# A planned two-layer kernel on one core: a one-element copy on another engine, another table of step order, and two buffers handed out differently

## The chip, the cores and the metric

The kernel runs on one core of a Trainium2 chip, which has eight. The metric is the device time of one execution in microseconds, as a median over several runs. A core has five engines that run side by side and wait for one another by semaphores: TensorE (PE: matmuls; PEld: weight loads), VectorE (DVE), ScalarE (ACT), GpSimd (POOL) and SyncE (SP). The last three can also issue DMA transfers. Each engine does its instructions strictly in the order in which they were issued to it: an instruction that waits holds up all that are queued behind it.

## The reference

Two layers on x of 2048 rows by 512 columns in bf16, each with its layer norm and its residual. The first is attention with 32 heads of 16 columns, in which each row sees 8 rows: itself and those 2, 4, ... 14 rows before it. The second is a gated network of width 1376.

```python
def _A_ref(x, wqkv, wo):
    H = 32; Dh = D // H
    W, dil = 8, 2
    q, k, v = qkv[0], qkv[1], qkv[2]
    idx = pos[:, None] - (jnp.arange(W) * dil)[None, :]
    ...
    logits = jnp.where(mask, einsum("bhsd,bhswd->bhsw", q, kg) * Dh ** -0.5, -1e9)
    o = einsum("bhsw,bhswd->bhsd", softmax(logits), vg)
    return o @ wo

def _B_ref(x, W_gate, W_up, W_down):
    gate, up = x @ W_gate, x @ W_up
    return ((gate * (gate > 0)) * up) @ W_down

h = x + _A_ref(_layernorm(x), wqkv, wo)
h2 = h + _B_ref(_layernorm(h), W_gate, W_up, W_down)
```

## The kernel before

The 2048 rows are worked in four chunks of 512. For each chunk `tk` the kernel makes the same steps, and a planner (`Plan`) interleaves the steps of all four. A step is one call of `add`: an engine, an assumed duration, the steps it depends on, the buffers that it takes and uses, and a function that issues its instructions. A step is named here as in the code, with its chunk behind a point: `xst.1` is the step `xst` of chunk 1. Steps of the first chunk's first layer norm also carry their block of 128 rows: `xxn1.0`.

The steps of a chunk, in the order of the data:

- First layer norm: `xst`, `xag` (VectorE, L473 and L476: statistics of one block of 128 rows and their aggregate), `xrl`, `xre` (ScalarE, L486 and L490: 1/sqrt by a logarithm and an exponential), `xnb` (VectorE, L494), `xxn` (the normalized rows; VectorE L521 in chunk 0, ScalarE L518 in the others). The rows are then turned so that columns lie on partitions: in chunks 0, 1 and 2 by TensorE (`xtp`, L550) and a copy out of PSUM (`xte` on ScalarE, L566; `xtv1` on VectorE, L564), in chunk 3 by DMA transposes on SyncE (`xtd`, L539, tile `quad<-row`).
- Query, key and value: twelve products of four matmuls each on TensorE (`qkv0` to `qkv11`, L591) and as many copies out of PSUM on ScalarE (`qe0` to `qe11`, L599). In chunk 0 the first six are cut by rows and by halves of the weights into `qka`, `qkd`, `qkb`, `qkc`, `qke`, so that they can begin when only a part of the input is there; `qka` and `qkd` need the first two of the four parts of the query and key weights, which `setup` loads with the transfers of L325 and L340.
- Scores: the products of queries and shifted keys on VectorE (`pr0`, `pr1`, L642; in chunk 0 in halves, L657: eight of them), summed over a head's columns by matmuls (`sc0`, `sc1`, L648, or after an addition on VectorE, `pa`, L692), the exponential on ScalarE (`ex0`, `ex1`, L706), and in chunk 0 a mask on VectorE (`mk0`, `mk1`, L709). `es` (VectorE, L738) adds the two halves, `den` (TensorE, L723) sums them, `dl` and `dr` (ScalarE, L729 and L732) make the reciprocal, and `am0`, `am1` (VectorE, L750) multiply by it in chunks 1 to 3.
- The weights of the attention are spread over the heads' columns by DMA broadcasts on SyncE: `bd0S` and `bd1S`, four transfers each (L766, tile `big<-ex`).
- `mu0` to `mu3` (VectorE, L798; in halves in chunk 0, L813) multiply them with shifted values. The eight products are then added in three levels; the first is an accumulating DMA on GpSimd (`ta`, L841, tile `big<-big`) for all but one of the sixteen, the others are on VectorE (`tree`, L801 and L835). In chunk 0 `om` (L805) multiplies by the reciprocal.
- The output projection `wo0` to `wo3` (TensorE, L879), the residual `rs` (VectorE, L890), the second layer norm (`hnm` L456, `hsq` L462, `hxn` L516; transposes `htp` or `htd`; `hrl` and `hre` make the factor that the very last step multiplies by).
- The gated network: `mm` (TensorE, L952 and L919), the copies out of PSUM `ue` and `ge` (ScalarE, L956 and L959), their product `gu` (VectorE, L980 and L929; `gtd` turns the last 96 columns by DMA), the second product `dn` (TensorE, L1002), the result `o` (ScalarE L1008 in chunks 0 and 1, followed by an accumulating DMA `oa`, L1031; VectorE L1010 in chunks 2 and 3) and the output transfer `os`. In the last chunk the last block of 128 rows is done in three parts of 256, 128 and 128 columns.

What sets the order is the list `RANK` (L18): its n-th entry is the rank of the n-th step that was added. `Plan.order` sorts by it, so on every engine the steps go out by rising rank. The planner's clock, with its assumed durations and arrival times (`XT`, `WT`), then says which buffer of a ring a step gets, and in which order the steps of different engines are written into the program; no instruction carries a time.

Three places beside the order play a part:

- The up and down weights are loaded late (`LATE`), because their place in SBUF must not be written too early. A tiny step `lg` (L859) writes four elements into the place of the up weights once the attention output of chunk 0 is complete; the transfers `ldu` (SyncE, L315) wait for it.
- `hsq` squares the centred rows on ScalarE; only the sum (`accum_out`) is used, and the squares go to a tile `junk` (L295) that nobody reads.
- The results `o` of chunks 2 and 3 go through a ring of five row buffers (`o_s`, L285), shared with two other uses.

Of the kernel before, what the change touches and what calls it, by code (L numbers as in the profile page):

```python
# [8 lines left out]
P = 128  # L9
# [50 lines left out]
class Op:  # L60
# [4 lines left out]
    def __init__(self, eng, dur, fn, deps=(), prio=0.0, take=(), use=(), lat=0.0, dq=None):  # L65
        self.eng, self.dur, self.fn, self.lat, self.dq = eng, dur, fn, lat, dq
        self.deps = [d for d in deps if d is not None]
        self.prio, self.take, self.use = prio, list(take), list(use)
        self.start = self.done = None


class Slots:
# [130 lines left out]
def kernel(  # L203
# [11 lines left out]
    nc = tc.nc  # L215
# [868 lines left out]
```

## Time and profile before

| | us |
|---|---|
| median of 3 runs | 195.03 |
| lowest and highest run | 194.85, 195.93 |
| the profiled execution, its own time | 195.59 |
| its span, from the first to the last instruction | 193.6 |
| TensorE, VectorE, ScalarE, GpSimd busy | 185.8, 150.2, 115.8, 22.9 |

The mean granted TensorE clock was 0.997. The profile is read in these views, all of the one profiled execution:

- the page's busy table (engine, busy time, share of the span, number of instructions), and its table of groups: line, engine, operation, what is written and read, shape, count, then busy time, the mean length of one in ns, and idle time ahead of it;
- the waits: an engine with tile and line, what it waited for, then the total in us, the number of waits and the longest;
- the chain of work that ended last: start, length, and what the time went to;
- the timeline: start, length, engine and line, operation, shapes, count of merged instructions; in brackets the idle time of the engine ahead of it and what ended that. "SPq" is SyncE's queue while it issues transfers;
- stretches: for each the length, then for TensorE, weight loads, VectorE, ScalarE and GpSimd the busy time with the count of instructions, then the clock, the share of the DMA engines, and GB/s;
- the answer for one tile or line: count, shortest, median and longest duration in ns, first and last start in us; for transfers the time from issue to landing.

A matmul of 512 columns is shown longer than the distance to the next, since matmuls are pipelined.

### The profile page before, as it was taken

What the parts mean: (1) busy time and instruction counts of PE and PEld (TensorE: products, weight loads), DVE (VectorE), ACT (ScalarE), POOL (GpSimd) and SP (SyncE); (2) the same over time, 40 slices, a digit from 0 to 9 for tenths busy, and PEclk for the clock granted to TensorE, in tenths of its full rate; (3) what the DMA queues carried; (4) which work ended last, traced back from release to release, by engine and by line L of the source; (5) the groups of instructions that cost most, each with busy time, mean ns of one, the idle gap of its engine ahead of it and who ended that gap; (6) DMA issues with size and microseconds to landing.
All of it is one profiled execution on the core that took longest, in us unless ns stands there. A gap on an engine that the chain in (4) does not pass through costs nothing.

```text
span 193.6 us, 3051 instructions
## 1 busy us (share of the span) xinstructions
PE 185.8 (96%) x1120; PEld 95.9 (50%) x1120; DVE 150.2 (78%) x245; ACT 115.8 (60%) x236; POOL 22.9 (12%) x35
## 2 busy tenths in 40 slices
PE   7599999899999999999999999999999999999993
PEld 7487454465446444544444445444554444554542
DVE  6699979999999999999999987898575720224343
ACT  3579897985839397861183798034595613475800
POOL 3000000330530033000064000017000000000000
PEclk9999999999999999999999999999999999999998
DMA  5898166795048859985559944759911150113013
GB/s 195 272 375 317 36 157 117 148 199 112 3 125 259 224 141 192 179 252 112 108 95 196 219 91 96 174 105 188 198 31 27 22 140 0 39 45 108 0 60 106
DMA packets 26734, 26.44 MB, mean 137 GB/s; under 512 B 12544, under 2 KB 22624, under 8 KB 26720
## 3 DMA queue, kind: packets, MB, share of 16 engines
q1 hardware_dynamic: 23264, 16.39, 30.9%
q0 software_dynamic: 2736, 8.91, 24.8%
q10 hardware_dynamic: 720, 0.95, 1.4%
q8 instruction: 9, 0.15, 0.3%
q14 instruction: 5, 0.04, 0.1%
HBM read 8.42 MB, written 2.10 MB: 54 GB/s over the span
## 4 chain that ended last, share of the span: by engine, by line
PE 82%; DMA 7%; ACT 5%; issue 2%; DVE 1%; SPq 0%; DVEq 0%
PE bank L952 35%; PE bank L591 16%; PE bank L1002 15%; PE bank L879 7%; PE bank L648 3%; DMA x_sm<-in_A_x_dram 3%; DMA quad<-row 3%; PE bank L919 3%; PE bank L550 2%; ACT vT L599 1%; DMA out_dram<-row 1%; ACT junk L462 1%; ACT row L518 1%; DVE row L1010 1%; ACT gr L959 1%
## 5 line engine op out<-in xcount | busy, mean ns | idle before, releaser
L952 PE MATMUL bank<-quad,wgu_sb 128*128 128x512 bf16 x320 | 71.9, 379 | 0.0
L952 PEld LDWEIGHTS <-wgu_sb 128*128 128x128 bf16 x320 | 30.9, 98 | 37.0 <-issue 1.3
L1002 PE MATMUL bank<-wd_sb,gT 128*128 128x512 bf16 (+3 forms) x198 | 39.4, 356 | 0.0
L956 ACT CAST up_sb<-bank 128x512 bf16<-128x512 f32 x40 | 22.7, 592 | 20.9 <-PE bank L952 11.7
L591 PE MATMUL bank<-quad,wqk_sb 128*128 128x512 bf16 (+2 forms) x176 | 29.9, 321 | 0.9 <-DMA quad<-row 0.9
L959 ACT ACTIVATE gr<-bank 128x512 bf16<-128x512 f32 x40 | 23.2, 606 | 9.5 <-PE bank L952 5.9
L980 DVE TENSOR_TENSOR gT<-gr,up_sb 128x1024 bf16<-128x1024 bf16 x20 | 13.8, 689 | 19.3 <-ACT gr L959 17.1
L1002 PEld LDWEIGHTS <-gT 128*128 128x128 bf16 (+1 forms) x198 | 18.4, 98 | 20.1 <-issue 0.4
L642 DVE TENSOR_TENSOR big<-quad,kT 128x4096 bf16<-128x4096 bf16 x11 | 24.9, 2289 | 0.1
L798 DVE TENSOR_TENSOR big<-big,vT 128x4096 bf16<-128x4096 bf16 x10 | 22.5, 2289 | 0.5 <-DMA big<-ex 0.5
L591 PEld LDWEIGHTS <-wqk_sb 128*128 128x128 bf16 x176 | 17.0, 113 | 11.5 <-issue 1.2
L841 POOL DMA_DIRECT2D big<-big x13 | 12.5, 985 | 63.8 <-DVE nb L494 31.6
L591 PE MATMUL bank<-quad,wv_sb 128*128 128x512 bf16 x64 | 16.0, 380 | 0.0
L879 PE MATMUL bank<-wo_sb,quad 128*128 128x512 bf16 x64 | 15.3, 380 | 0.0
L1008 ACT ACTIVATE up_sb<-bank,iv 128x512 bf16<-128x512 f32 x8 | 5.1, 684 | 16.3 <-PE bank L1002 16.3
L801 DVE TENSOR_TENSOR big<-big 128x1024 bf16<-128x1024 bf16 (+2 forms) x19 | 12.1, 660 | 3.4 <-DMA big<-big 3.3
L890 DVE SCALAR_TENSOR_TENSOR x_sm<-x_sm,bank 128x512 bf16<-128x512 bf16 x16 | 10.7, 683 | 3.0 <-PE bank L879 3.0
L462 ACT ACTIVATE junk<-x_sm,mv 128x512 bf16<-128x512 bf16 x16 | 11.7, 731 | 1.5 <-DVE mv L456 1.5
L473 DVE BATCH_NORM_STATS2 st<-x_sm 128x6 f32<-128x512 bf16 x16 | 10.1, 682 | 2.0 <-DMA x_sm<-in_A_x_dram 2.0
L813 DVE TENSOR_TENSOR big<-big,vT 128x2048 bf16<-128x2048 bf16 x8 | 9.3, 1219 | 1.4 <-DMA big<-ex 1.4
L599 ACT CAST quad<-bank 128x512 bf16<-128x512 f32 x16 | 9.1, 590 | 2.1 <-PE bank L591 2.1
L518 ACT ACTIVATE row<-x_sm,nb,rs 128x512 bf16<-128x512 bf16 x12 | 9.8, 815 | 0.3 <-DVE nb L494 0.3
(80 smaller groups left out, 173.6 us busy)
## 6 DMA issues: line engine op xcount, KB each, us to landing
big<-big POOLq DMA_DIRECT2D x13, 512.0 KB, 5.9
big<-ex SPq DMA_DIRECT2D x32, 128.0 KB, 2.8
wgu_sb<-in_B_W_gate_dram SPq DMA_DIRECT2D x2, 688.0 KB, 9.9
wgu_sb<-in_B_W_up_dram SPq DMA_DIRECT2D x2, 688.0 KB, 4.7
wd_sb<-in_B_W_down_dram SPq DMA_DIRECT2D x2, 640.0 KB, 4.6
x_sm<-in_A_x_dram SPq DMA_DIRECT2D x2, 512.0 KB, 5.9
wqk_sb<-wqk_sb POOLq DMA_DIRECT2D x2, 512.0 KB, 6.6
x_sm<-up_sb POOLq DMA_DIRECT2D x4, 256.0 KB, 4.9
```

What stands on the lines that cost most here:

```text
L462: nc.scalar.activation(out=junk[:], in_=h.t[:] if h else x_sm[:, tk * BPC + j, :], func=ACT.Square, bias=mv.t[:, j, 0:1], scale=1.0, accum ...
L591: nc.tensor.matmul(mm.t[:, lo:hi], lhsT=wv_sb[:, dt, t:D:NT] if c == 2 else wqk_sb[:, dt, c * D + t:(c + 1) * D:NT], rhs=xnT.t[:, dt, lo:h ...
L642: V.tensor_tensor(out=pb.t[:].rearrange("p (t w) s -> p t w s", t=2), in0=q4, in1=k4, op=ALU.mult)
L798: V.tensor_tensor(out=mt.t[:], in0=ab.t[:], in1=v8, op=ALU.mult)
L801: V.tensor_tensor(out=mt.t[:, 0:n, :], in0=mt.t[:, 0:n, :], in1=mt.t[:, n:2 * n, :], op=ALU.add)
L841: nc.gpsimd.dma_start(mt.t[:, 0:4, :], mt.t[:, 4:8, :], accum_op=ALU.add)
L879: nc.tensor.matmul(od.t[:], lhsT=OT.t[:, t, j * P:(j + 1) * P], rhs=wo_sb[:, t, :], start=(t == 0), stop=(t == NT - 1 and tk not in RPE))
L952: nc.tensor.matmul(mm.t[:fs, lo:hi], lhsT=wgu_sb[:, dt, g, ft * P: ft * P + fs], rhs=hnT.t[:, dt, lo:hi], start=(dt == 0), stop=(dt == NT ...
L956: nc.scalar.copy(out=ub.t[:fs, i, :], in_=um.t[:fs, :])
L959: nc.scalar.activation(out=gr.t[:fs, i, :], in_=gm.t[:fs, :], func=ACT.Relu)
L980: V.tensor_tensor(out=gt.t[:fs, 0:n, :], in0=gr.t[:fs, 0:n, :], in1=ub.t[:fs, 0:n, :], op=ALU.mult)
L1002: nc.tensor.matmul(od.t[:, c0:c1], lhsT=gts[ft].t[:fs, ft % 2, j * P:(j + 1) * P], rhs=wd_sb[:fs, ft, c0:c1], start=(ft == 0), stop=(ft == ...
```

## The change

Four things in the program are different.

1. `lg`, the four-element copy that releases the transfer of the up weights, is on VectorE instead of GpSimd.
2. `RANK` is another list. Of each engine's queue some steps are where they were and most have moved; the first ones, and the places that matter later, are listed below.
3. `junk` has two halves, and `hsq` writes them in turn.
4. In chunks 2 and 3 a result takes a row buffer per block of 128 rows; so the three parts of the last block share one, where each had its own.

In the planner, `order` with a list takes one step at a time over all engines, where it took the lowest rank of each engine and among these the earliest by its clock. Its model knows two more waits, for the landing of the eighth transfer before (`hw`, `flight`) and between some key copies and score products (`near`), and has other arrival times in `XT` and `WT`. These bear on which buffer a step gets and on the order of writing, not on the instructions.

```diff
 RANK = [
     1, 2, 3, 4, 5, 6, 7, 8, 9, 10, 18, 11, 12, 13, 14, 15, 16, 17, 0, 19,
-    21, 23, 24, 27, 31, 34, 35, 20, 26, 28, 32, 37, 40, 44, 49, 22, 25, 30, 33, 39,
+    21, 24, 26, 29, 33, 37, 36, 20, 22, 25, 27, 31, 35, 40, 39, 23, 28, 30, 32, 44,
...
@@ def order
-        waiting = list(self.ops)
+        self.flight = [9.0, 9.4, 11.5, 12.9, 14.9, 16.2, 17.9, 19.6]
+        waiting = sorted(self.ops, key=lambda o: (o.prio, o.seq), reverse=True) if RANK else list(self.ops)
...
-            for op in ([q[-1] for q in queues.values() if q] if queues else waiting):
+            for op in (waiting[-1:] if RANK else waiting):
...
+                for d in op.near:
+                    if d.done is not None:
+                        t = max(t, d.done + (self.HOP if d.eng != op.eng else 0.0))
+                for n in range(op.hw):
+                    t = max(t, self.flight[n - 8] - 0.63 * n + self.HOP)
...
-    junk = sb.tile([P, CS], BF16, name="junk")
+    junk = sb.tile([P, 2, CS], BF16, name="junk")
...
-    XT = (3.5, 3.65, 4.4, 6.1, 6.7, 7.7, 8.7, 9.1, 13.0, 14.5)
-    WT = (8.2, 8.2, 6.3, 10.8, 16.0, 25.5, 19.6, 29.0)
+    XT = (3.1, 3.25, 4.1, 5.9, 7.15, 8.65, 9.0, 9.4, 12.9, 14.85)
+    WT = (8.35, 8.35, 7.0, 11.5, 16.15, 25.5, 19.6, 29.0)
...
-                        nc.scalar.activation(out=junk[:], in_=h.t[:] if h else x_sm[:, tk * BPC + j, :],
+                        nc.scalar.activation(out=junk[:, j % 2, :], in_=h.t[:] if h else x_sm[:, tk * BPC + j, :],
...
             def f_lg(OT=OT):
-                nc.gpsimd.tensor_copy(out=wgu_sb[0:1, :, 1, 0:1], in_=OT.t[0:1, :, 0:1])
+                V.tensor_copy(out=wgu_sb[0:1, :, 1, 0:1], in_=OT.t[0:1, :, 0:1])
-            lg = add(("lg", tk), "POOL", 0.2, f_lg, list(oev.values()), apr, use=[OT], lat=0.1)
+            lg = add(("lg", tk), "DVE", 0.08, f_lg, list(oev.values()), apr, use=[OT], lat=0.1)
...
             if tk not in ODA:
-                ob = Buf(o_s)
+                if j != BPC - 1 or c0 == 0:
+                    ob = Buf(o_s)
...
-                    take=[ob], use=[od, iv], lat=DL)
+                    take=[ob], use=[od, iv, ob], lat=DL)
```

What the two lists make of the queues (a bar sets off groups; where four steps have one name, they are the four blocks or the halves):

```
TensorE, start
before  warm xtp0 fill xtp1 xtp2 | qka3 qka2 qka5 qka4 xtp3 qka1 qkd3 qkd4 qkb4 ...
after   warm xtp0 xtp1 fill | qka5 qka4 qka0 qka1 qka3 qkd0 xtp2 qkd4 qka2 xtp3 qkd1 qkb1 qkd5 qkb0 qkc0 qke0 ...

VectorE, to the masks of chunk 0
before  xst0 xst1 xag0 xst2 xag2 xag1 xxn0 xst3 xag3 xxn1 xxn2 xxn3 xtv1 | xst.1 x4 xag.1 x4
        pr1a xnb.1 pr0a pr1c pr0c pr0a pr0c pr1c pr1a mk0 | xst.3 x4 xag.3 mk1 xag.3 x3
after   xst0 xst1 xag0 xag1 xst2 xag2 xxn0 xxn1 xst3 xag3 xtv1 xxn2 xxn3 | xst.1 x2 xag.1 xst.1 x2 xag.1 x3
        pr1a pr0a xnb.1 pr0a pr0c pr0c pr1c pr1a mk0 pr1c | xst.3 x4 mk1 xag.3 x4

VectorE, from there to the attention output of chunk 0
before  xst.2 x2 xnb.3 xst.2 x2 xag.2 mu1a xag.2 x3 mu0a mu3a mu1c es xnb.2 mu2a mu2c mu0c mu3c
        pr0.1 tree1 tree1 tree2 om1 tree2 pr1.1 om2 tree3 pr0.1 tree0 tree3 tree0 om3 om0 pr1.1 pr1.2
after   xst.2 x2 xnb.3 xst.2 x2 xag.2 x2 mu1a xag.2 x2 mu0a mu2a xnb.2 mu1c mu3c mu2c mu3a mu0c es
        pr0.1 tree1 tree1 om1 pr0.1 tree2 tree0 tree2 pr1.1 tree0 pr1.1 tree3 om0 tree3 om2 om3 pr1.2 lg

TensorE, around the first product of chunk 3
before  ... the twelve of chunk 1, den.0 | qkv1.3
after   ... eleven of chunk 1 with xtp.2 behind it, qkv0.1, xtp.2 | qkv4.3 qkv5.3 qkv11.3 qkv6.3 xtp.2 den.0 xtp.2 qkv1.3

TensorE, output projections of chunks 0 and 3
before  sc0.1 wo1.0 wo3.0 sc1.1 wo2.0 wo0.0 den.1    ...  mm4.2 wo1.3 mm1.2 wo0.3 mm4.2 wo2.3 dn2.2 wo3.3
after   sc1.1 wo1.0 wo0.0 wo2.0 den.1 wo3.0          ...  wo0.3 mm2.2 mm0.2 wo1.3 mm4.2 wo3.3 mm5.2 wo2.3

SyncE
before  bd0S.0 bd1S.0 xtd.3 x4 ldu x2 bd1S.1 bd0S.1 ...  os1.0 bd1S.3 gtd.1 bd0S.3
after   bd0S.0 bd1S.0 xtd.3 x4 ldu x2 bd0S.1 bd1S.1 ...  gtd.1 bd1S.3 bd0S.3

GpSimd, chunk 3 (ta) and the output accumulations of chunk 1 (oa)
before  ta2.3 oa3.1 ta0.3 oa1.1 ta1.3
after   ta1.3 ta0.3 oa1.1 ta2.3 oa3.1
```

More of the change, by code (lines that the diff above doesn't have):

```diff
@@ L19 @@
     1, 2, 3, 4, 5, 6, 7, 8, 9, 10, 18, 11, 12, 13, 14, 15, 16, 17, 0, 19,
[37 rows of a table removed]
[37 rows of a table added]
 ]
 class Op:
-    __slots__ = ("eng", "dur", "lat", "dq", "fn", "deps", "prio", "take", "use", "start", "done", "seq", "key")
+    __slots__ = ("eng", "dur", "lat", "dq", "fn", "deps", "prio", "take", "use", "start", "done", "seq", "key", "near", "hw", "first")
     def __init__(self, eng, dur, fn, deps=(), prio=0.0, take=(), use=(), lat=0.0, dq=None):
@@ L69, in __init__ @@
         self.start = self.done = None
+        self.near, self.hw, self.first = [], 0, False
 class Slots:
@@ L115, in order @@
     def order(self):
-        waiting = list(self.ops)
+        self.flight = [9.0, 9.4, 11.5, 12.9, 14.9, 16.2, 17.9, 19.6]
+        waiting = sorted(self.ops, key=lambda o: (o.prio, o.seq), reverse=True) if RANK else list(self.ops)
         free = {}
-        queues = None
-        if RANK:
-            queues = {e: [] for e in ("PE", "DVE", "ACT", "SP", "LD", "POOL")}
-            for op in sorted(waiting, key=lambda o: (o.prio, o.seq), reverse=True):
-                queues[op.eng].append(op)
         left = len(waiting)
@@ L183, in order @@
                 op.done = at + op.lat
+            self.flight += [op.done - 0.63 * (op.hw - 1 - n) for n in range(op.hw)]
             free[op.eng] = max(t + op.dur, held)
@@ L194, in order @@
             left -= 1
-            if queues:
-                queues[op.eng].pop()
-            else:
-                waiting.remove(op)
+            waiting.remove(op)
         return sorted(self.ops, key=lambda o: (o.start, o.seq))
@@ L666 @@
                             apr, take=[pb], use=[qT], lat=DL)
+                    a.first = t == 0
                     prd.append((a, pb, f_sc))
@@ L766, in f_bd @@
                             q.dma_start(ab.t[:, w0 + w, :], ex.t[w * HB:(w + 1) * HB, :].unsqueeze(1).to_broadcast([HB, 4, CS]))
-                    abd.append(add(("bd%d%s" % (hf, eng[0]), tk), eng, len(ws) * BDI[eng[0]], f_bd, [exd[hf]], apr + 1,
+                    abd.append(add(("bd%d%s" % (hf, eng[0]), tk), eng, len(ws) * BDI[eng[0]] + (0.35 if tk == 0 else 0), f_bd, [exd[hf]], apr + 1,
                                    take=[ab], use=[exs[hf]], lat=0.77,
@@ L1039 @@
             b = add(("o%d" % n, tk), "DVE", D5 * share + (0.05 if share < 1 else 0), f_o, [a] + ivd, mb - 200,
-                    take=[ob], use=[od, iv], lat=DL)
+                    take=[ob], use=[od, iv, ob], lat=DL)
             add(("os%d" % n, tk), "ACT" if last else "SP", 0.4, f_os, [b], mb + 6, use=[ob], lat=0.55, dq=(0.3, 0.4 * share))
+    for o in plan.ops:
+        n = o.key[0] if o.key else ""
+        if o.dq and o.eng in ("SP", "ACT"):
+            o.hw = 4 if n[:2] == "bd" else 2 if n == "ldd" and o.dur > 0.5 else 1
+        if n in ("qe1", "qe5"):
+            o.near = [p for p in plan.ops if p.key and p.key[0] in ("pr0", "pr1") and 0 < p.key[1] < o.key[1] and (n == "qe1") == p.first]
+            for p in o.near:
+                p.near.append(o)
     todo = plan.order()
```

72 rows, old and new, of the table RANK are left out of this document.

## The prediction

> **What bounds the kernel now.** I read the page's busy table first, then TensorE's waits, the chain, and the timeline where TensorE waits.
>
> ```profile
> span 193.6 us, 3051 instructions
> PE 185.8 (96%) x1120; PEld 95.9 (50%) x1120; DVE 150.2 (78%) x245; ACT 115.8 (60%) x236; POOL 22.9 (12%) x35
> ...
> L952 PE MATMUL bank<-quad,wgu_sb 128*128 128x512 bf16 x320 | 71.9, 379 | 0.0
> ```
> ```profile
> PE bank L550 <- DVE row L521: 2.2, 2, 1.9
> ...
> PE bank L591 <- DMA quad<-row: 0.9, 1, 0.9
> PE bank L723 <- DVE row L738: 0.4, 1, 0.4
> ```
> ```profile
> 36.00:190.00 154.00, 154.00 (x852) 74.69 (x851) 118.58 (x175) 88.86 (x183) 20.01 (x19) 1.00 0.56 122
> ```
> ```profile
> 190.00:194.00 4.00, 0.29 (x6) 0.11 (x3) 0.61 (x2) 0.00 (x0) 0.00 (x0) 0.80 0.31 93
> ```
> ```profile
> 32.40 2.61 DMA quad<-row
> 35.01 0.14 issue
> ...
> 98.02 13.81 PE bank L952 x64
> ...
> 187.29 2.72 DMA out_dram<-row
> ```
>
> In the window rows the second number is TensorE's busy time: 154.00 of 154.00 us from 36 to 190, at granted clock 1.00, and its last matmul ends at 190.29. The chain's 64 matmuls take 13.81 us, 0.2158 each, one behind the other, though the profile models each as 0.379 long. So nothing can be won behind 36 us, only lost. What can be won are the waits ahead: 1.9 us before the transpose at 8.48, and 0.4 + 0.9 between 33 and 35.15. In these last two the modelled ends hide 0.379 - 0.216 = 0.16 each, so about 1.7 us are idle there. Some 3.6 us is the most that any order could save.
>
> **Which work ends these two waits.**
>
> ```profile
> 5.33 0.38 DVE L521 TENSOR_SCALAR row<-x_sm,mv,rs 128x512 bf16<-128x512 bf16 x1
> ...
> 7.21 0.69 DVE L473 BATCH_NORM_STATS2 st<-x_sm 128x6 f32<-128x512 bf16 x1 [1.50 <-DMA x_sm<-in_A_x_dram]
> ...
> 8.04 1.09 DVE L521 TENSOR_SCALAR row<-x_sm,mv,rs 128x512 bf16<-128x512 bf16 x3
> ...
> 8.48 0.72 PE L550 MATMUL bank<-identity,row 128*128 128x128 bf16 x8 [1.86 <-DVE row L521]
> ...
> 9.95 2.47 DVE L473 BATCH_NORM_STATS2 st<-x_sm 128x6 f32<-128x512 bf16 x4 [0.48 <-DMA x_sm<-in_A_x_dram]
> ...
> 12.62 1.19 DVE L657 TENSOR_TENSOR big<-quad,kT 128x2048 bf16<-128x2048 bf16 x1
> ...
> 13.80 8.03 DVE L657 TENSOR_TENSOR big<-quad,kT 128x2048 bf16<-128x2048 bf16 x7
> ...
> 21.75 0.16 DVE L709 TENSOR_TENSOR ex<-ex,mask 128x16 bf16<-128x16 bf16 x1
> ...
> 21.82 2.47 DVE L473 BATCH_NORM_STATS2 st<-x_sm 128x6 f32<-128x512 bf16 x4
> ...
> 21.93 6.36 SPq L766 DMA_DIRECT2D big<-ex  x8
> ...
> 22.86 1.06 PE L591 MATMUL bank<-quad,wv_sb 128*128 128x512 bf16 x4
> ...
> 28.39 5.38 SPq L539 DMA_TRANSPOSE quad<-row  x4
> ...
> 28.60 1.23 DVE L813 TENSOR_TENSOR big<-big,vT 128x2048 bf16<-128x2048 bf16 x1 [1.44 <-DMA big<-ex]
> ...
> 35.15 1.03 PE L591 MATMUL bank<-quad,wqk_sb 128*128 128x512 bf16 x4 [0.93 <-DMA quad<-row]
> ```
>
> At 7.21 VectorE stands at xst3.0, waiting for a block of x; xxn1.0, whose input is there, is queued behind it, and TensorE waits for xxn1.0. At 35.15 TensorE has no product of chunk 1 left and needs chunk 3's four DMA transposes. These stand on SyncE behind the eight broadcasts of chunk 0, which start at 21.93, right after the mask mk0.0 (21.75), which VectorE does only after all eight products (12.62 to 21.8). So VectorE's order sets when TensorE runs dry.
>
> **The change part by part.** The order follows from RANK: sorted by it, the steps of an engine give its queue.
>
> *Start.* VectorE's queue becomes xst0 xst1 xag0 xag1 xst2 xag2 xxn0 xxn1 xst3: xxn1.0 no longer waits for the late block. xxn0 ends near 5.7 as before, xxn1 near 6.1, so its transpose runs at 6.2. Next TensorE wants qka5, which needs the second row of query and key weights:
>
> ```profile
> L325 ACTq DMA_DIRECT2D wqk_sb<-in_A_wqkv_dram x3: 452/453/468, 1.2 to 2.2; - x3
> ...
> DMA to landing us min/median/max: 3.3/6.2/6.4
> ```
>
> The median is the second of three, issued near 1.7: it lands near 7.85. Five qka steps (ten matmuls of 0.057) run to 8.45; qkd0 needs xtv1.0, behind xst3.0 and its aggregate, so 8.55; xtp2 follows at about 9.0, xtp3 at 9.45. By 9.7 TensorE has done eight of the small steps instead of four (4 x 0.115 = 0.46 us ahead). I give 0.1 back at qke0, which waits for xte3: the start brings 0.36, and chunk 1's first product goes from 22.86 to 22.5.
>
> *VectorE to the first mask.* After xst3.0 (7.9): aggregate, copy, two normalizations, to 9.2; then four statistics and four aggregates, which took 9.95 to 12.62 = 2.67. First product near 12.05 instead of 12.62 (11.9 by the sum, and qe1.0 ends near 12.0). Products follow at (8.03-0.08)/7 = 1.136 us. The new queue puts mk0.0 behind seven, not eight: 12.05 + 7 x 1.136 + 0.07 for xnb.1 = 20.1 instead of 21.75. Its inputs keep up: the last pr0 ends at 17.8, sc0.0 stands on TensorE at 18.0, ex0.0 ends near 20.0.
>
> *SyncE.* bd0S.0 from 20.25 (2.6 us, or 3.7 with the one long issue that made 8 issues 6.36 us); bd1S.0 waits for mk1.0: 20.2 + 1.14 (eighth product) + 2.4 (four xst.3) = 23.9, so 24.0 to 26.6. The transposes start at 26.65 instead of 28.39. From the first issue to the last landing they took 35.01 - 28.39 = 6.62; they land at 33.3. Their rows xxn.3 come from ScalarE in one stretch from about 25.6, 0.72 us apart, earlier than needed.
>
> *TensorE to the transposes.* From 22.5: twelve products of chunk 1 (48 x 0.2158 = 10.36) and two xtp.2 (0.45) that the new queue puts ahead of the first product of chunk 3: 33.3. Transposes and TensorE arrive together; I take 33.4. Behind it the work of before, 190.29 - 35.15 = 155.14 us, less 0.45 (xtp.2 done) plus 0.22 (den.0 still to do): 154.9. End 188.3 instead of 190.29: **2.0 us gained**.
>
> *What must keep up.* VectorE was busy 36 to 110 almost without a gap, so it must shift as much. mu1a.0 stood 1.44 us for a broadcast. VectorE would have reached it at 27.16, 2.87 behind mk1.0 (21.82 + 2.47 = 24.29); with mk1.0 at 23.9 that is 26.8, and bd0S.0 is out by 24: no wait.
>
> ```profile
> 49.75 0.76 DVE L805 TENSOR_TENSOR quad<-big,rec 128x512 bf16<-128x512 bf16 x2
> 50.42 4.49 DVE L642 TENSOR_TENSOR big<-quad,kT 128x4096 bf16<-128x4096 bf16 x2
> ```
>
> From mu1a.0 to the last input of the output projection VectorE took 50.51 - 28.60 = 21.9; the new queue has one more of the long products in it (4.49 / 2 = 2.2) and some 0.4 of waits less: om3.0 ends at 50.5. TensorE reaches wo1.0 at 50.8 (33.4 and 23 of its steps): 0.3 in hand. By the same sums sc1.2, wo2.1 and sc0.3 have 0 to 0.3 in hand, wo0.3 0.3 to 1. For a slip at the tightest I take **0.3 us**; bounds: 0 and the whole 2.0.
>
> *Release of the up weights.*
>
> ```profile
> L952 PE MATMUL bank<-quad,wgu_sb x22: 378/380/389, 63.5 to 70.0; 128*128 128x512 bf16 x22
> L315 SPq DMA_DIRECT2D wgu_sb<-in_B_W_up_dram x2: 394/424/453, 55.0 to 55.4; - x2
> L859 POOL COPY wgu_sb<-quad x1: 4395/4395/4395, 50.6 to 50.6; 1x4 bf16<-1x4 bf16 x1
> ...
> DMA to landing us min/median/max: 4.1/4.7/5.3
> ```
>
> Four elements took GpSimd 4.395 us: until both of VectorE's products that began at 50.42 were over. On VectorE it stands behind pr1.2 (52.7), about 0.15 us as its smallest operations; the weights land near 58.6, TensorE wants them at 61.6. Before they landed 55.4 + 5.3 = 60.7 for 63.5. Covered on both sides: 0. Without the cover each us late is a us of TensorE.
>
> The Trainium skill (SBUF — State Buffer, Who interferes with whom) has the loser of the port that VectorE and GpSimd share blocked for one whole instruction. By that the copy would have ended behind the first product, at 52.7; the row says behind both, 54.96. By either the weights are in time and the sum stays.
>
> *The discarded squares* go to two halves in turn: that can save ScalarE time alone, of which 193.6 - 115.8 = 77.8 us are free, and TensorE waits for none of it from 36 on: 0. *The last row block's three parts* share one buffer:
>
> ```profile
> 190.13 0.61 DVE L1010 SCALAR_TENSOR_TENSOR row<-bank,iv,x_sm 128x128 bf16<-128x128 f32 x2 [0.28 <-DMA out_dram<-row]
> ```
>
> The first of these two waited 0.28 us for an output transfer to free a buffer; sharing removes that, but the second needs TensorE's last matmul (190.29) anyway. Bounds: -0.28 and, should the last part wait until the transfer of the part before it has landed, +2.7 (the chain's 2.72 at 187.29). The parts are different columns, so I take 0.
>
> **Sum.** The profiled execution took 195.59 us, span 193.6; 2.0 - 0.3 = 1.7 off gives 193.9. It lies 0.56 above the median of the runs, 195.03, which is taken as the base, since the waits are the same work: **193.3 us**.
>
> **Rivals.**
>
> *A. The transposes land no earlier (35.0).* For it: ex0.0, mk0.0, mk1.0 and xxn.3 cross four engines, each with a few tenths in hand. Against: the eight products were one unbroken block, so their order decides. TensorE then stands from 33.3 to 35.15 and keeps only xtp.2 ahead: 0.45 - 0.22 = 0.2 gained, 194.8.
>
> *B. VectorE becomes the bound.* Should mu1a.0 wait for its broadcast as before (1.44), om3.0 ends at 51.9 and TensorE stands 1.1 us at wo1.0, with the same lag at later handoffs: 2.0 - 1.1 = 0.9, 194.1. For it speaks the full window 36 to 110; against, that even with the one long issue the broadcasts are out 2.8 us before their use (24.0 and 26.8).
>
> *C. Slower: the last chunk's output projection.*
>
> ```profile
> 126.03 8.90 DVE L798 TENSOR_TENSOR big<-big,vT 128x4096 bf16<-128x4096 bf16 x4 [0.51 <-DMA big<-ex]
> ...
> 142.03 0.69 DVE L801 TENSOR_TENSOR big<-big 128x1024 bf16<-128x1024 bf16 x1 [0.42 <-DMA big<-big]
> ```
> ```profile
> 147.44 0.86 PE bank L879 x4
> ```
> ```profile
> DMA to landing us min/median/max: 4.6/6.4/9.0
> ```
>
> The chain's row is wo1.3, the first of the last chunk's output projection. The new queue puts wo0.3 first and at about 140.5, eight places earlier among TensorE's steps, and everything on TensorE stands behind it. It needs the last of three accumulating transfers on GpSimd's queue (landings in the last fence), after which VectorE went on at 142.03, 16.0 behind the first product of the stage (126.03). VectorE should be 2.0 us ahead there, and the transfer gtd.1, which stood between the two groups of the stage's broadcasts on SyncE, goes ahead of both (1.3, as the transposes: 5.38 / 4): that product starts between 122.7 and 124.0. I take 123.2, the last landing at 139.2, and with two additions (1.0) wo0.3 can go at 140.2. If the stage starts no earlier than before, it goes at 143.0, TensorE stands 2.5 us, and 195.03 - 2.0 + 2.5 = 195.5; with the longest landing of the row (9.0 against 6.4) 2.6 more, 198.1. It decides from a lag of 2.3 us. Against it: one of the two output accumulations that lay between the three is moved behind them.
>
> The Trainium skill (Trainium Kernel Development and Optimization, Key Constraints) says that transfers from SyncE, ScalarE and GpSimd share the same 16 DMA engines and interleave, so that an earlier broadcast meets other transfers; the spread 4.6 to 9.0 agrees with that, and it speaks for C.
>
> *D. The new queue does nothing*, as when the block of x lands before xst3.0 and the transposes are hidden: 195.0. The waits above speak against it.
>
> **Chances.** Forecast (192.4 to 193.9) 0.48, B 0.15, A with D 0.14, C and any like it 0.23. A measurement of this kernel tells about 0.5% (0.98 us) from no change, so faster means below 194.05. The forecast and about two thirds of B's spread lie below: 0.58. Within: 0.05 of B, 0.13 of A and D, and 0.05 of C, its low end: 0.23. Above 196.0: 0.18 of C, 0.01 of A: 0.19. Range 192.4 (the whole 2.0, the buffer's 0.28 and 0.3 more of the first wait) to 195.9 (A, B, the low end of C, and the forecast with the whole 2.7 of the shared buffer). The forecast's own range is 192.4 to 193.9.
>
> **What would show it.** Right: the first mask near 20, the transposes issued near 26.7 with TensorE's wait for them under 0.3; VectorE's wait for the broadcast gone; the copy on VectorE under 0.2 us; TensorE's last matmul near 188.3 to 188.6; no wait of TensorE behind 36 above 0.3. Wrong: a wait at L879 (B at 51, C at 140), transposes still issued after 28, or a wait of L952 for up weights. A late first block of x alone would move start and end alike and prove nothing.

## The result and the profile after

The changed kernel took 192.87 us, the median of 6 runs (192.65 to 193.43). The kernel before, run beside it, took 196.4 (194.85 to 197.55); three of its six runs are those behind the 195.03 of the base, three took 196.87 to 197.55, and the ratio, which is of fast runs alone, is 0.9898, with a 95% interval of 0.9863 to 0.9933. The predicted 193.3 us was 0.9911 of that 195.03. Repeated later, with more runs of before beside it, the changed kernel gave 192.89 (ratio 0.9926, interval 0.9902 to 0.9951) and 192.97 (0.9913, 0.988 to 0.9947). So by the three ratios it is faster by 1.4 to 2.0 us, and the forecast was 1.7.

The head and the busy times of the changed kernel's page, and then TensorE's waits in full (us in total, times, longest):

```profile
span 190.7 us, 3053 instructions
## 1 busy us (share of the span) xinstructions
PE 186.1 (98%) x1120; PEld 96.5 (51%) x1120; DVE 149.5 (78%) x246; ACT 115.3 (60%) x236; POOL 18.5 (10%) x34
```
```profile
PE bank L428 <- DVE warm L326: 1.0, 1, 1.0
```

Both waits ahead of 36 us that the prediction wanted to win are gone from the list, the one for VectorE's rows and the one for the transposes. What is left stands ahead of the first matmul. The windows of the changed kernel from 36 to the last matmul, and from 36 to 110 (columns: busy time in total, TensorE, weight loads, VectorE, ScalarE, GpSimd, clock, DMA share, GB/s), show where it has nothing more to give:

```profile
36.00:187.00 151.00, 151.00 (x830) 72.76 (x828) 115.11 (x174) 85.19 (x178) 14.04 (x17) 1.00 0.54 121
36.00:110.00 74.00, 74.00 (x432) 35.27 (x431) 73.59 (x94) 47.70 (x98) 9.71 (x12) 1.00 0.72 159
```

TensorE is busy all the way to 187.0 at clock 1.00, as it was to 190 before; in the second row VectorE is busy for 73.59 of the 74 us as well. The timeline of the changed kernel from the start to the first product of chunk 3:

```profile
6.12 0.72 PE L549 MATMUL bank<-identity,row 128*128 128x128 bf16 x8
...
6.30 0.69 DVE L472 BATCH_NORM_STATS2 st<-x_sm 128x6 f32<-128x512 bf16 x1
...
11.06 2.36 DVE L656 TENSOR_TENSOR big<-quad,kT 128x2048 bf16<-128x2048 bf16 x2 [0.18 <-ACT kT L598]
...
19.09 0.16 DVE L709 TENSOR_TENSOR ex<-ex,mask 128x16 bf16<-128x16 bf16 x1
19.16 1.22 DVE L656 TENSOR_TENSOR big<-quad,kT 128x2048 bf16<-128x2048 bf16 x1
...
19.27 6.13 SPq L766 DMA_DIRECT2D big<-ex  x8
...
21.21 1.05 PE L590 MATMUL bank<-quad,wv_sb 128*128 128x512 bf16 x4
...
22.68 0.15 DVE L709 TENSOR_TENSOR ex<-ex,mask 128x16 bf16<-128x16 bf16 x1
...
25.50 5.23 SPq L538 DMA_TRANSPOSE quad<-row  x4
...
25.61 1.19 DVE L813 TENSOR_TENSOR big<-big,vT 128x2048 bf16<-128x2048 bf16 x1
...
32.09 1.89 PE L590 MATMUL bank<-quad,wqk_sb 128*128 128x512 bf16 x8
```

Read it against the rows of before in the prediction. The two first transposes run as one group of eight matmuls at 6.12; they ran at 5.77 and 8.48. The fourth block's statistics (6.30) no longer wait, because that block was early in this execution, as told below. The first mask is at 19.09 with one product behind it (21.75 before, all eight ahead of it), SyncE's eight broadcasts start right behind it, the transposes go out at 25.50 instead of 28.39, and TensorE meets them at 32.09 with no wait behind the row, where it stood 0.93 us at 35.15. VectorE's first product with a broadcast, 25.61, has no wait either; it had 1.44.

This execution is earlier than forecast at every one of these places, by some 1.1 us (25.50 for 26.65, 32.09 for 33.4, the last matmul at 187.18 for 188.3). Its loads were: the fourth block of x, awaited at 7.19 in the profile of before, had landed at 5.30 here, from an issue at 1.69 (1.67 before). A profile is one execution, so what follows sets executions with like landings side by side where it reads times off traces.

### The profile page after: what moved, and what is told of

The parts are those of the page before. It is cut to its first block, busy times and chain, and to the rows that moved or that the text cites. A ratio compares the mean times of both kernels' runs of the same rounds, so it can differ in the third digit from the quotient of the medians.

```text
span 190.7 us, 3053 instructions
## 1 busy us (share of the span) xinstructions
PE 186.1 (98%) x1120; PEld 96.5 (51%) x1120; DVE 149.5 (78%) x246; ACT 115.3 (60%) x236; POOL 18.5 (10%) x34
## 4 chain that ended last, share of the span: by engine, by line
PE 95%; DVE 2%; DMA 1%; issue 0%
PE bank L952 36%; PE bank L590 22%; PE bank L1003 20%; PE bank L879 7%; PE bank L647 3%; PE bank L919 3%; PE bank L549 2%; DMA x_sm<-in_A_x_dram 1%; DVE st L472 1%; PE bank L692 1%; PE bank L723 0%; PE bank L436 0%; DVE mv L475 0%; DVE row L1011 0%; DVE row L520 0%
## 5 line engine op out<-in xcount | busy, mean ns | idle before, releaser
L952 PE MATMUL bank<-quad,wgu_sb 128*128 128x512 bf16 x320 | 72.7, 379 | 0.0
L798 DVE TENSOR_TENSOR big<-big,vT 128x4096 bf16<-128x4096 bf16 x9 | 20.2, 2280 | 0.0
L841 POOL DMA_DIRECT2D big<-big x12 | 11.2, 1019 | 37.6 <-PE bank L590 29.8
L801 DVE TENSOR_TENSOR big<-big 128x1024 bf16<-128x1024 bf16 (+2 forms) x18 | 11.5, 652 | 0.1
L1011 DVE SCALAR_TENSOR_TENSOR row<-bank,iv,x_sm 128x512 bf16<-128x512 f32 (+2 forms) x10 | 6.2, 640 | 6.8 <-PE bank L1003 6.8
L598 ACT CAST kT<-bank 128x512 bf16<-128x512 f32 x16 | 9.2, 592 | 3.2 <-DVE big L641 3.2
L598 ACT CAST vT<-bank 128x512 bf16<-128x512 f32 x16 | 9.4, 595 | 2.0 <-PE bank L590 2.0
```

Of the source, the lines that this page charges most:

```text
L598: nc.scalar.copy(out=o, in_=mm.t[:])
L798: V.tensor_tensor(out=mt.t[:], in0=ab.t[:], in1=v8, op=ALU.mult)
L801: V.tensor_tensor(out=mt.t[:, 0:n, :], in0=mt.t[:, 0:n, :], in1=mt.t[:, n:2 * n, :], op=ALU.add)
L952: nc.tensor.matmul(mm.t[:fs, lo:hi], lhsT=wgu_sb[:, dt, g, ft * P: ft * P + fs], rhs=hnT.t[:, dt, lo:hi], start=(dt == 0), stop=(dt == NT ...
```

## The experiments

The twelve runs came in three groups, each with its own runs of before: 194.94 us (35 runs), 194.56 (26) and 194.54 (19).

**The two parts without the order.** The copy alone, in the kernel before:

```diff
-                nc.gpsimd.tensor_copy(out=wgu_sb[0:1, :, 1, 0:1], in_=OT.t[0:1, :, 0:1])
+                V.tensor_copy(out=wgu_sb[0:1, :, 1, 0:1], in_=OT.t[0:1, :, 0:1])
...
```

> The kernel before with one part of the change, the release copy on VectorE. If the order alone earns the gain: within 0.3 us of before, the copy 0.16 us instead of 4.4, the up weights landing some 4 us earlier than 60.7, and nobody who waits for them. If the freed release earns it: at least 1 us faster.

Measured: 195.49 us, ratio 1.0014 (0.9981 to 1.0047). It gives nothing that can be told.

The halves of `junk` and the shared row buffer alone, in the kernel before:

```diff
-                        nc.scalar.activation(out=junk[:], in_=h.t[:] if h else x_sm[:, tk * BPC + j, :],
+                        nc.scalar.activation(out=junk[:, j % 2, :], in_=h.t[:] if h else x_sm[:, tk * BPC + j, :],
...
-                ob = Buf(o_s)
+                if j != BPC - 1 or c0 == 0:
+                    ob = Buf(o_s)
```

> The kernel before with the two halves for the discarded squares and the shared row buffer alone. Order theory: within 0.3 us of before; the 0.28 us wait of the last output rows for a buffer is gone, the end moves by 0.1 at most. Rival: the buffers earn 0.3 us or more, or the shared buffer makes a part wait for a transfer, up to 2.7 us slower.

Measured: 194.59 us, ratio 0.9966 (0.9939 to 0.9994). The interval just leaves 1 out. By the ratio that is 0.7 us, by the medians 0.35, and by the interval's upper end 0.1, so the rival's 0.3 us is neither shown nor ruled out. Its trace shows no gain at the end: from the last matmul (189.08) to the end of the span it took 3.73 us, 3.27 in the profile of before. The run does not tell the two buffers apart.

**The order undone.** The changed kernel with the list of before:

```diff
-    21, 24, 26, 29, 33, 37, 36, 20, 22, 25, 27, 31, 35, 40, 39, 23, 28, 30, 32, 44,
+    21, 23, 24, 27, 31, 34, 35, 20, 26, 28, 32, 37, 40, 44, 49, 22, 25, 30, 33, 39,
...
```

> The changed kernel with the list of before: release on VectorE, both buffers and the new planner stay, the queues are those of before. Order theory: the time of before within 0.5 us, and TensorE idle about 1.7 us again between 33 and 35. If the planner's new choice of buffers matters: 1 us or more away from before, either way.

Measured: 196.17 us, ratio 1.0046 (1.0014 to 1.0077). TensorE's waits in it:

```profile
PE bank L590 <- DMA quad<-row: 0.6, 1, 0.6
PE bank L549 <- DVE row L520: 0.5, 1, 0.5
PE bank L723 <- DVE row L738: 0.3, 1, 0.3
PE bank L647 <- DVE big L656: 0.2, 1, 0.2
```

(The 1.0 us ahead of the first matmul is left out of this list and of three of those below.) The wait for the transposes is back; with what the modelled ends hide it is 0.76 us, where 1.7 was expected. Against the repeats of the changed kernel (0.9926 and 0.9913) the list is worth 1.2 to 1.3%, 2.3 to 2.6 us, more than the whole change: with the old list, the changed program is 0.9 us slower than before, outside the 0.5 of the expectation and short of the 1 us of its rival. In its trace TensorE loses 0.41 us behind the matmul at 20.7, 0.30 behind that at 51.8 and 0.49 behind that at 54.8, which it did not lose before. That the new model, which hands out the buffers, does not suit the old list is the likely reason; no run tried it. So not all of the 2.3 to 2.6 us need be the new list's own gain.

The kernel before once more, for the scatter:

> The kernel before, unchanged, once more. Ratio 1.000 within 0.3%. In its trace the point is when the fourth block of x lands: 7.2 us in the profile of before, 5.3 in that of the changed kernel, from transfers that are issued alike. If it varies from run to run, up to 1 us of the 2.8 us between the two spans is not the change's; if it is 7.2 again, it belongs to the kernel.

Measured: 195.25 us, ratio 1.0022 (0.9989 to 1.0056), with the same two waits of TensorE (2.2 and 0.9 us in its list). The fourth block landed at 7.28, again late; by the expectation that speaks for the kernel, but two other runs with the old list had it at 6.20 and 6.69. The execution is no twin of the first profile all the same: its first mask came at 22.97 instead of 21.75, and its last matmul ended at 191.01 instead of 190.29. The page's row of granted clock (40 equal slices of the span, in tenths) dips where TensorE's first products stand:

```profile
PEclk9889999999999999999999999999999999999999
```

From 8.15 to 11.57 us the clock was 0.50; in the profile of before it was 1.00 there.

**The changed kernel again**, as the base of the next three:

> The changed kernel, unchanged, once more, beside before on one chip. Ratio 0.985 to 0.992 (1.6 to 2.9 us). In the trace no wait of TensorE behind 9 us, whenever the loads land.

Measured: 192.89 us, ratio 0.9926 (0.9902 to 0.9951), just above the expected 0.992. The first products of chunk 3 start at 32.15, behind 0.16 us of idle time where none was expected: the transposes had landed at 32.02.

**The copy back on GpSimd**, in the changed kernel (the first diff of this section, reversed).

> The changed kernel with the release copy back on GpSimd. Order theory: within 0.3 us of the changed kernel; the copy is held as long as VectorE works on products of two SBUF inputs, from 49.7 to 51.8 or 52.2, about 2.2 to 2.6 us, and the up weights still land by 58.5 for a use at 60.5. If the release on VectorE earns the gain: 1 us or more slower than the changed kernel.

Measured: 193.32 us, ratio 0.9935 (0.991 to 0.996); 0.4 us above the repeat where 0.3 was the bound, with overlapping intervals (two of its seven runs took 193.15 us or less, and seven of the repeat's eight), and no wait of TensorE for up weights:

```profile
PE bank L428 <- DVE warm L326: 1.0, 1, 1.0
PE bank L590 <- DMA wqk_sb<-in_A_wqkv_dram: 0.6, 1, 0.6
PE bank L549 <- DVE row L520: 0.2, 1, 0.2
PE bank L590 <- DMA quad<-row: 0.2, 1, 0.2
```
```profile
L859 POOL COPY wgu_sb<-quad x1: 2531/2531/2531, 50.6 to 50.6; 1x4 bf16<-1x4 bf16 x1
```

The last three are not in the profile of after, and all lie ahead of 34 us, before the copy runs at 50.6; the copy can't have made them. They come from late loads: in this execution the fourth block of x landed at 7.20, as in the profile of before (7.19). So up to 50 us this is the changed order under the loads of before, just the comparison that the profile of after could not give. Its timeline:

```profile
7.22 0.69 DVE L472 BATCH_NORM_STATS2 st<-x_sm 128x6 f32<-128x512 bf16 x1 [0.85 <-DMA x_sm<-in_A_x_dram]
...
11.98 2.36 DVE L656 TENSOR_TENSOR big<-quad,kT 128x2048 bf16<-128x2048 bf16 x2
...
20.01 0.16 DVE L709 TENSOR_TENSOR ex<-ex,mask 128x16 bf16<-128x16 bf16 x1
...
22.14 1.05 PE L590 MATMUL bank<-quad,wv_sb 128*128 128x512 bf16 x4
...
26.48 5.41 SPq L538 DMA_TRANSPOSE quad<-row  x4
...
33.29 1.89 PE L590 MATMUL bank<-quad,wqk_sb 128*128 128x512 bf16 x8 [0.15 <-DMA quad<-row]
```

VectorE again waits for the late block, but with the second normalization done, and TensorE with its first transposes waits instead for the second row of weights (until 8.03, in the list above).

**The start undone.** The changed kernel, with the statistics of the fourth block back ahead of the second normalization in VectorE's queue (by four numbers of `RANK`):

```diff
-xst2 xag2 xxn0 xxn1 xst3 xag3
+xst2 xag2 xxn0 xst3 xxn1 xag3
```

> The changed kernel with one step put back: the statistics of the fourth block stand ahead of the second block's normalization again, as in before. If TensorE is bound by nothing else behind its start: 0.4 to 1.0 us slower than the changed kernel, the delay of its first small products (0.5 us with an early block, 1.3 with a late one) seen again at the end. If VectorE's later order sets the time alone: within 0.2 us.

Measured: 193.72 us, ratio 0.9954 (0.9932 to 0.9977), 0.8 us above the repeat. The intervals overlap a little; of the runs themselves, side by side on one chip, seven of the repeat's eight took 193.15 us or less, and four of these twelve. TensorE's waits in it:

```profile
PE bank L549 <- DVE row L520: 1.2, 2, 0.7
```

There are two waits again, as before. Its loads were early (fourth block at 5.71, 5.76 in the repeat), and its last matmul ends at 187.57 against 187.16: 0.4 us by the traces, 0.8 by the medians.

**The first mask undone.** The changed kernel, with the eighth product ahead of the first mask in VectorE's queue:

```diff
-pr1a mk0 pr1c
+pr1a pr1c mk0
```

> The changed kernel with the first mask behind all eight products again, as in before. As the prediction had it, this mask sets the broadcasts and so the transposes: 1.1 us later, TensorE stands 0.8 us at the first product of chunk 3, 0.8 us slower. Rival, read from the changed kernel's trace: the second mask sets them, since the second four broadcasts wait for it at 22.86 while the first four are out by 21.9; then the transposes start 0.1 to 0.2 later and the time stays within 0.3 us.

Measured: 193.82 us, ratio 0.9958 (0.9927 to 0.9989), 0.9 us above the repeat; these intervals overlap too, but only one of the twelve runs took 193.15 us or less. Its waits of TensorE and its timeline:

```profile
PE bank L590 <- DMA quad<-row: 1.1, 1, 1.1
```
```profile
20.77 0.15 DVE L709 TENSOR_TENSOR ex<-ex,mask 128x16 bf16<-128x16 bf16 x1
...
23.23 0.15 DVE L709 TENSOR_TENSOR ex<-ex,mask 128x16 bf16<-128x16 bf16 x1
...
27.29 5.25 SPq L538 DMA_TRANSPOSE quad<-row  x4
...
33.90 1.89 PE L590 MATMUL bank<-quad,wqk_sb 128*128 128x512 bf16 x8 [1.10 <-DMA quad<-row]
```

Its loads were late (6.83). The nearest landing with the new order is 6.75, in the first of the two runs that were to have more products (below). Against it the first mask is 1.21 us later (20.77 and 19.56), the transposes 1.38 (27.29 and 25.91), the products of chunk 3 also 1.38, and the last matmul 1.26 (188.92 and 187.66). One product moved by one place puts back TensorE's wait for the transposes.

The rival of that expectation fell, but by a narrow way. The second mask was there at 23.38, and had the fourth broadcast's issue lasted 0.6 us like its neighbours, the fifth could have gone out near 23.6 and the transposes near 26.2, only 0.3 later than in the other run. That issue lasted 1.64 us, and the fifth went out at 24.69. Such a long issue, 0.97 to 1.75 us, stands among the first eight in all seven traces in which the first mask is behind all products, and in none of the seven with the early mask (0.71 at most). So about 1.1 of the 1.4 us at the transposes comes through this issue; why it goes with the order is open.

**The start alone**, in the kernel before:

```diff
-xxn0 xst3 xag3 xxn1 xxn2
+xxn0 xxn1 xxn2 xst3 xag3
```

> The kernel before with one thing of the new order: the second and third normalization of chunk 0 stand ahead of the fourth block's statistics in VectorE's queue. Theory (the start is a separate gain only if the transposes come earlier too): TensorE's wait near 6.4 goes from about 2 us to under 0.5, chunk 1's first product comes 0.3 to 1 us earlier, but the first mask still stands behind all eight products, so TensorE's wait for chunk 3's transposes near 33 to 35 grows by what the start saved, less what the eight products themselves come earlier; the time is within 0.5 us of before (ratio 0.997 to 1.002). Rival (the start is a gain by itself, because VectorE's products and with them mask, broadcasts and transposes start earlier by as much): 0.5 us or more faster, ratio 0.997 or less.

Measured: 194.43 us, ratio 0.9995 (0.9967 to 1.0023): nothing, as the theory had it. TensorE's waits in it, and its transpose of the fourth block:

```profile
PE bank L550 <- DVE row L521: 1.5, 2, 1.0
...
PE bank L591 <- DMA quad<-row: 0.6, 1, 0.6
```
```profile
9.18 0.40 PE L550 MATMUL bank<-identity,row 128*128 128x128 bf16 x4 [0.99 <-DVE row L521]
```

The way there is not the theory's. The wait at the start fell from 2.2 to 1.5 us only, not under 0.5, because TensorE's queue, unchanged, asks for the fourth transpose after eight small matmuls and then waits for its row. The first product of chunk 1 starts at 22.49, no earlier than in the run with the buffers alone (22.29, fourth block at 6.69, here at 6.57), and the wait for the transposes fell from 0.9 to 0.6 where it should have grown. So the run does not show a gain at the start being eaten by the second wait: this pair shows no gain at the start. The likely reason is that VectorE's step pays only together with TensorE's new queue, which puts query and key steps ahead of the third and fourth transpose; the new queue without that step is the run with the start undone, and it loses.

**More work on VectorE.** Two runs were to add six and sixteen small products to VectorE at 49.6 us:

```diff
                 V.tensor_tensor(out=OT.t[:, t, :], in0=mt.t[:, 0, :], in1=rc.t[:], op=ALU.mult)
+                if t == 1 and tk == 0:
+                    for _ in range(6):
+                        V.tensor_tensor(out=warm[:], in0=mt.t[:, 0, 0:P], in1=rc.t[:, 0:P], op=ALU.mult)
```

> The kernel after, with six more VectorE products of 128x128 right behind the normalizing product of the second quad of chunk 0 (near 50 us); their result is not used. At some 0.12 us each they put about 0.7 us of work into VectorE's queue at the handoff to the output projection that starts at 49.6. Theory (VectorE is level with TensorE there, nothing in hand): TensorE gets a wait of about the added time at that projection or at a handoff behind it, and nothing behind 36 us gives it back: the time is 0.5 to 0.8 us above after (193.4 to 193.7, ratio to before 0.995 to 0.998). Rival (VectorE has a few tenths in hand at each later handoff and the added work is swallowed): within 0.2 us of after.

> As the run with six added VectorE products, with sixteen of them (about 1.9 us). Theory (VectorE is level with TensorE): the cost grows one to one, 1.6 to 2.0 us above after (194.5 to 194.9), and all that the new order won is gone. Rival (there is slack of s us in VectorE's queue): the cost is the added time less s, and six and sixteen products together give s.

Both tell nothing of VectorE's slack. The function is called after the loop over the chunks has moved on, so `tk` is no longer 0 there and not one product was added; the page of the first shows the instruction count of the changed kernel:

```profile
span 191.2 us, 3053 instructions
```

They are two more runs of the changed kernel: 193.07 us, ratio 0.9914 (0.9881 to 0.9947), and 193.12, 0.9925 (0.9897 to 0.9953). In the first the fourth block of x landed late, at 6.75, which makes a second comparison under like loads. How much slack VectorE has between 36 and 110 us stays open.

> The changed kernel once more, as the base of the two runs with added VectorE work: 192.9, no wait of TensorE above 0.5 us except behind its first matmul.

Measured: 192.97 us, ratio 0.9913 (0.988 to 0.9947). TensorE waits 0.7 us for the first normalized row at 5.99, a little more than the 0.5 expected, and still ends its last matmul at 187.11.

## Why the prediction was right

By executions with like landings (us, from the traces; "repeat" is the run that was to have six more products):

| | predicted | before (old order) | copy on GpSimd (new) | buffers only (old) | repeat (new) |
|---|---|---|---|---|---|
| fourth block of x lands | 7.2 | 7.19 | 7.20 | 6.69 | 6.75 |
| first mask | 20.1 | 21.75 | 20.01 | 21.06 | 19.56 |
| first product of chunk 1 | 22.5 | 22.86 | 22.14 | 22.29 | 21.69 |
| transposes issued | 26.65 | 28.39 | 26.48 | 27.34 | 25.91 |
| TensorE goes on with chunk 3 | 33.4 | 35.15 | 33.29 | 33.93 | 32.52 |
| last matmul ends | 188.3 | 190.29 | 188.30 | 189.08 | 187.66 |
| span | 191.9 | 193.56 | 191.86 | 192.81 | 191.22 |

(The predicted span is 193.6 less 1.7.) Landings alone do not fix the rest. Two more executions with the old order landed much as the profile of before did: with the copy on VectorE alone at 7.42, where the last matmul ended at 189.91, 0.4 earlier, and the kernel before once more at 7.28, where it ended at 191.01, 0.7 later, with the lowered clock shown above. So a pair is good to some 0.4 us, and to 0.7 with such a clock. That the first pair meets the forecast to 0.02 at the last matmul is luck in part: the forecast was worked out from that very profile of before, whose long issue of 1.75 us was the longest of all.

- *Start: right in kind, under-sized.* The prediction gave it 0.36 us; the two pairs show 22.86 - 22.14 = 0.72 and 22.29 - 21.69 = 0.60. The step that was off is the time of the third and fourth transposes: eight small steps were to be done by 9.7, and in the run with the copy on GpSimd the fourth transpose (9.28) is out and the eight steps are done by 9.50; the 0.1 given back at qke0 does not show. That the second row of weights would hold TensorE till about 7.85 is that run's wait until 8.03. The start alone is worth nothing (0.9995); without it the change loses 0.4 to 0.8 us.
- *First mask and transposes: right.* The chain of the prediction, mask to broadcasts to transposes to TensorE, holds to 0.2 us in the column of the copy on GpSimd, and putting back one product breaks it at the place named. In the prediction's own sum the second mask came only 0.4 us earlier (23.9 for 24.29); most of the 1.74 us of the transposes was the long issue of before, which it let run out ahead of that mask. In the traces with the early mask no long issue came at all. From chunk 1's first product to the first of chunk 3 it saves 1.14 and 0.81 us, where 1.39 was forecast: against the forecast TensorE came 0.4 earlier to transposes that came only 0.2 earlier, so the gain at the start takes its share from this one. So the start was sized too small and this part too large by about as much, and their sum came out.
- *Behind 33 us: the 0.3 us in the wrong place.* From the first product of chunk 3 to the end TensorE took 155.14 us before, 155.01 with the copy on GpSimd and 155.09 after; 154.9 was forecast. Of the 0.3 us allowed for slips at tight handoffs only 0.1 to 0.2 shows ahead of the last matmul, but the span gives 0.3 back behind it: from the last output's landing to the end it is 1.35 us before (192.21 to 193.56) and 1.69 after (189.04 to 190.73). So the last 0.3 us of the net 1.7 is luck: the size is right for a reason that the prediction did not have. The spans of the two pairs are 1.70 and 1.59 apart.
- *The tight handoffs (rivals B and C).* The prediction had om3.0 end at 50.5 and wo1.0 at 50.8. In the profile of after TensorE is 1.2 us ahead of that and VectorE 0.9 (VectorE's rows, then TensorE's):

```profile
48.88 0.75 DVE L805 TENSOR_TENSOR quad<-big,rec 128x512 bf16<-128x512 bf16 x2
...
138.03 0.43 DVE L835 TENSOR_TENSOR quad<-big 128x512 bf16<-128x512 bf16 x1
```
```profile
49.60 1.69 PE L879 MATMUL bank<-wo_sb,quad 128*128 128x512 bf16 x7
```
```profile
139.39 1.03 PE L879 MATMUL bank<-wo_sb,quad 128*128 128x512 bf16 x4
```

  VectorE's last rows for the first projection end at 49.63, as TensorE begins it: no lag, and no margin that the rows show, where the prediction had 0.3 in hand. The last chunk's first projection has its input at 138.46 and starts at 139.39, 0.9 us in hand, inside the 0.3 to 1 of the prediction; C did not come, since VectorE did run ahead there.
- *The copy, the squares, the row buffer.* Priced at nothing. The copy takes 0.157 us on VectorE, and the up weights go out at 51.9 instead of 55.0:

```profile
L859 DVE COPY wgu_sb<-quad x1: 157/157/157, 51.8 to 51.8; 1x4 bf16<-1x4 bf16 x1
```

  Both runs of it agree with nothing (1.0014, and 0.4 us in the other, with overlapping intervals and no wait for it in the trace). The buffers may have something in them (0.9966, 0.9939 to 0.9994), at the edge of what can be told; nothing in the traces shows where. In the changed kernel the output's wait for a buffer is gone, and the last part waits for TensorE alone, as argued:

```profile
187.22 0.35 DVE L1011 SCALAR_TENSOR_TENSOR row<-bank,iv,x_sm 128x128 bf16<-128x128 f32 x1 [0.23 <-PE bank L1003]
```

  Nothing waits for the transfer of the part before it, so the 2.7 us at the other bound did not come.

Rival A, the transposes no earlier, is what one product moved by one place brings back in part. Rival D fell with the start and the mask undone. The range's upper end, 195.9, is 0.1 short of the 193.3 + 2.7 that it names; nothing came near it.

## What to carry to other kernels

Where one engine is busy from some point to the end, only idle time ahead of that point can be won; find each wait there and follow it back over the queues to the step that releases it, since moving that step by one place in another engine's queue (here a 0.16 us mask ahead of a 1.14 us product) can be worth nearly a microsecond. Releasing a wait earlier pays only if the waiting engine's own queue asks next for something that is there: here two queues had to change together, and one alone gave nothing. Before a profile is held against another at a start that waits for loads, compare when the loads landed and what clock was granted; five executions of the changed program differed by 1.45 us in one landing and by 0.55 at the last matmul.

## What the runs showed of the hardware

- *Landing of the first loads.* The fourth block of x, issued at 1.67 to 1.70 us in all of these executions, landed at 5.30, 5.76, 5.96, 6.06 and 6.75 in five of the changed kernel and at 7.20 with the copy put back on GpSimd; in the old order at 6.20 to 7.42. In the new order the last matmul stays at 187.11 to 187.22 for the first four and then follows: 187.66 and 188.30. Part of the 3.1 us between the first two profiles (190.29 and 187.18) is this. The two groups overlap; whether the order has a share in the landings is open.
- *A lowered clock with the old start.* In kernels whose VectorE does the fourth block's statistics ahead of the second normalization, 19 of 140 runs had a mean granted clock of 0.981 to 0.991 (195.88 to 198.97 us); in the kernels with the new start all 65 had 0.995 or more. The one such run that was traced, the kernel before once more, had 0.50 from 8.15 to 11.57 us, and TensorE's wait for the second row ended in it, at 8.57. Why the two go together is open.
- *A small GpSimd copy beside VectorE.* Four elements took 4.395 us while two of VectorE's 128x4096 products ran and 2.531 us while one did. It ended at 54.96 and 53.14, each time about 0.13 us after VectorE had begun its first instruction that reads a PSUM bank (54.82 and 53.01 in its timelines), behind products that read and write SBUF only. The Trainium skill (SBUF — State Buffer, Who interferes with whom) says of VectorE's two-port modes that whoever issues first gets the port pair shared with GpSimd for the whole instruction while the other blocks, and that an instruction with two SBUF inputs, as these products are, contends with GpSimd's reads as well. If the copy were blocked for the one instruction that ran at its issue, it would agree with neither case: in the second too another VectorE instruction, of 0.41 us, ran between the product and the copy's end. Two cases show this, and none was made for it.
- *Eight broadcasts held SyncE for 5.6 to 6.4 us in every order.* The lines of SyncE's issues, of before and then of after (ns min/median/max of one issue):

```profile
L766 SPq DMA_DIRECT2D big<-ex x32: 548/602/1753, 21.9 to 123.2; - x32
```
```profile
L766 SPq DMA_DIRECT2D big<-ex x32: 544/595/663, 19.3 to 119.0; - x32
```

  Before, one of the first eight lasted 1.75 us. After, none did, but the fifth waited for the second mask (22.68 and 0.15 long, issued at 22.86), as predicted; the eight took 6.36 and 6.13 us. The other traces divide in the same way: one long issue with the late mask, none with the early one. What makes an issue long is not known.
- *The end of the program.* The 1.69 us behind the last landing stand in seven executions with the new order (1.68 to 1.71) and 1.32 to 1.35 in those with the old one, but also in the run with the late mask (1.32). In six of the seven the difference lies between GpSimd's last two semaphore instructions (0.42 to 0.43 us apart, 0.06 in the others). Nothing in the traces explains it.
